# Layer 1's low halves placed 128 bytes further on in SBUF

## The chip, the cores and the metric

One core of one Trainium2 chip. The metric is the device time of one execution in microseconds, and of several runs their median.

## The reference, cut to what matters

Block-causal attention over 4 batches, 8 heads, 576 positions and head size 64; its output, 2,304 tokens of 512 channels, goes through two layers. Layer 1, where the change lies, is `h = x @ w_in` (512 to 2,048), softplus, and `@ w_out` (2,048 to 512):

```
attn = softmax(mask(q @ k.T / 8)) @ v
h = x @ w_in
g = maximum(h, 0) + log1p(exp(-abs(h)))
x2 = g @ w_out
```

Layer 2 (512 to 1,024 to 512, with a softmax-weighted unit and a layer norm between) follows on x2.

## The kernel before, in words

Every float32 operand of a layer's matrix product is split into a high half, rounded to float32r, and a low half, the rest. A product is then three matmuls into the same PSUM tile: high by high, high weights by low input, low weights by high input.

**Layer 1.** The tokens are cut into nine chunks of 256. For each chunk `Pair` works on two of the 16 blocks of 128 hidden columns at a time, 72 pairs in all. `Pair.a` (called twice) makes 12 matmuls each into `hp` with `w1` as the stationary and `xt` as the moving operand of 256 columns. ACT makes abs, exp and ln of it, DVE joins them (`stt`), a copy makes `gh`, and `do_gl` subtracts it to make `gl`. `Pair.b` (called twice) makes 12 matmuls each with `w2` as the stationary operand and `gh` or `gl` as the moving one, into `acc` (for chunk 1 into `R`). The loop of `Pair.a`, which `Pair.b` repeats with `gh`, `gl` and `w2`, is

```
for k in range(4):
    mm(hp[:, j], w[:, 0, k, :], x[:, 0, k, :], ...)
    mm(hp[:, j], w[:, 0, k, :], x[:, 1, k, :], ...)
    mm(hp[:, j], w[:, 1, k, :], x[:, 0, k, :], ...)
```

So of three matmuls the middle one moves a low half. Each matmul has a weight load of its own, and the load for the next matmul runs while the present one streams its columns. All matmuls are recorded at line 236, the helper `mm`.

**Order.** The order of all instructions on all engines is worked out when the program is built: `Plan` places tasks on the engines by rank, estimated duration and due time. The change touches no task, no duration and no rank, so the order stays.

**Stages.** Up to about 100 us: attention over the first 256 positions of the first batches (`UnitA`), the loading and unpacking of layer 1's weights (`Piece`, from `raw`), and what pairs of the first chunks these let through. To about 200 us: the rest of the first two chunks and of `UnitA`. To about 465 us: attention over the other positions (`UnitC`) between the pairs of the next chunks. To about 561 us: the last pairs, with layer 2's first blocks among them. To the end: layer 2 (`Tok`), whose matmuls move 512 columns, the last 48 of them 256.

**Places.** The tile pools are stacks in each partition's bytes. On the left side, from low to high: `w` (all layer weights but the first four blocks of `w1`), `l1` (`t`, `gh`, `gl`, `stg`, small ones), `xt` (three buffers of 8,192 bytes) and `wx` (the first four blocks of `w1`). Small unused tiles (`pad_x`, `pad_l`, spare columns of `gcol`) shift what follows. The places that come out of this, in bytes of a partition: `w1` from 4,224 and from 161,664, `w2` from 53,376, 102,528 and 110,976, `gh` at 123,968 and 126,016, `gl` at 128,064 and 130,112, `xt` at 137,024, 145,216 and 153,408. All blocks within them step by multiples of 512.

Call the *distance* of a matmul the start of the weights that are loaded while it streams (those of the next matmul) less the start of what it moves, modulo 256 bytes. Weights of layer 1 start at 128 modulo 256, and all that moves at 64, so the distance is 64 in every matmul of layer 1. In layer 2 the moving operands (`u1`, and `w1` tiles that hold the second matrix) and the stationary ones start at the same residue: distance 0.

Of the kernel before, what the change touches and what calls it, by code (L numbers as in the profile page):

```python
# [10 lines left out]
F32 = mybir.dt.float32  # L11
F32R = mybir.dt.float32r
# [54 lines left out]
CT = 256  # L67
# [159 lines left out]
def body(ctx: ExitStack, tc: tile.TileContext, qk, qkA, vP, vA, w1, w2, u1, u2, gln, out):  # L227
# [3 lines left out]
    XTB, LAG = 3, 3  # L231
# [21 lines left out]
    def pool(name, side, **kw):  # L253
        return tc.tile_pool(name=name, bufs=1, side=side, reuse_waits="tile", **kw)
# [4 lines left out]
    pl1 = left.enter_context(pool("l1", "left"))  # L259
    early, xts = ExitStack(), ExitStack()  # L260
    pxt = xts.enter_context(pool("xt", "left"))
    px = early.enter_context(pool("wx", "left"))
    qsh = psl.enter_context(pool("qh", "left", space=PSUM))
    state = {}
# [68 lines left out]
    xt = {}  # L333

    def xt_of(c):
        if c not in xt:
            xt[c] = pxt.tile([128, 2, 4, CT], F32R, tag="xt", name="xt", bufs=XTB)
            if len(xt) == XTB:
                pxt.tile([128, 16], F32, name="pad_x")
        return xt[c]  # L340
# [14 lines left out]
    class UnitC:  # L355
# [169 lines left out]
        def x_hi(self, c, off, done, w, e):  # L525
            copy(e, xt_of(c)[:, 0, self.pr, off:off + w], self.xn[:, done:done + w])
# [6 lines left out]
    class UnitA:  # L533
# [131 lines left out]
        def x_hi(self, e):  # L665
            copy(e, xt_of(self.b)[:, 0, self.pr, :], self.o)
# [7 lines left out]
    class Pair:  # L674
# [65 lines left out]
            copy(e, self.gh, self.t)  # L740

        def do_gl(self):
            self.gl = pl1.tile([128, 2, CT], F32R, tag="gl", name="gl", bufs=2)
            DVE.tensor_sub(self.gl, self.t, self.gh)  # L744

# [80 lines left out]
    def open_q():  # L826
        psl.close()
        state["qtr"] = left.enter_context(pool("qtr", "left", space=PSUM))
        pl1.tile([128, 24], F32, name="pad_l")

    NR, NCA = 3, 4
    t_open = add("POOL", 500, 0.0, open_a, ())
# [11 lines left out]
    def w_of(t, i):  # L844
        return lambda: t[:, i]
# [7 lines left out]
    for kind, f in todo:  # L853
        src, t, done = (w1[f], w1t[f], w1ready) if kind == "w1" else (w2[f * 128:f * 128 + 128, :], w2t[f], w2ready)
        p = Piece(src, w_of(t, 0), w_of(t, 1))
# [17 lines left out]
    def u1_of(i, f):  # L873
        return lambda: state["u1"][i][:, :, f * 128:f * 128 + 128]
# [4 lines left out]
    for f in range(8):  # L879
        p = Piece(u1[f], u1_of(0, f), u1_of(1, f))  # L880
# [4 lines left out]
    for f in range(8):  # L885
        p = Piece(u2[f * 128:f * 128 + 128, :], w_of(w1t[6 + f], 0), w_of(w1t[6 + f], 1), gcol[:, f:f + 1])
        n = len(upieces) % 3
        plan.at_group("U2", f)
        p.plan(upieces, 0.0, conv_u, 3 if f > 2 else n + 1, 3 if f > 2 else n + 1, [t_u, t_2], w1_free(6 + f))
        u2d.append(p.t_lo)  # L890
    t_q = add("PE", 1, 0, open_q, evacs[NCH - 1] + [pairs[-1].t_b1, t_u])
    t_w = add("DVE", 1, 0, open_3, [pairs[-1].t_a1, t_2])

# [225 lines left out]
```

## Time and profile before

| | |
|---|---|
| median of 3 runs | 753.29 us (751.56 to 753.55) |
| the profiled execution, its own time | 751.01 us |
| its span, first to last instruction | 749.2 us |
| matmuls | 5,368, of them 3,456 of layer 1 with 256 columns |
| mean granted clock of TensorE | 0.998 |

The span is the time from the first to the last instruction; the profiled execution's own time has 1.8 us around it. PE is TensorE's matmuls, PEld its weight loads; the ends of matmuls are modelled, so it is the step from one start to the next, or the length of a run of back-to-back matmuls in the chain of waits, that tells what one costs.

### The profile page before, as it was taken

What the parts mean: (1) busy time and instruction counts of PE and PEld (TensorE: products, weight loads), DVE (VectorE), ACT (ScalarE), POOL (GpSimd) and SP (SyncE); (2) the same over time, 40 slices, a digit from 0 to 9 for tenths busy, and PEclk for the clock granted to TensorE, in tenths of its full rate; (3) what the DMA queues carried; (4) which work ended last, traced back from release to release, by engine and by line L of the source; (5) the groups of instructions that cost most, each with busy time, mean ns of one, the idle gap of its engine ahead of it and who ended that gap; (6) DMA issues with size and microseconds to landing.
All of it is one profiled execution on the core that took longest, in us unless ns stands there. A gap on an engine that the chain in (4) does not pass through costs nothing.

```text
span 749.2 us, 13919 instructions
## 1 busy us (share of the span) xinstructions
PE 728.7 (97%) x5368; PEld 648.0 (86%) x5368; DVE 580.7 (78%) x1185; ACT 421.6 (56%) x876; POOL 0.7 (0%) x6
## 2 busy tenths in 40 slices
PE   7789999999999999999999999999999999999998
PEld 4688999999988888888878889999998888888887
DVE  5999994367787878877677886765879998998882
ACT  5788874354777767676666764446642433333331
POOL 0000000000000000000000000000000000000000
PEclk9999999999999999999999999999999999999999
DMA  7666630102476687648667662316313554433332
GB/s 224 202 219 199 235 118 23 57 22 72 87 159 146 139 153 165 140 112 166 120 136 160 143 130 96 114 58 198 127 43 99 116 111 99 98 98 84 85 64 77
DMA packets 153762, 91.66 MB, mean 122 GB/s; under 512 B 123360, under 2 KB 136928, under 8 KB 153696
## 3 DMA queue, kind: packets, MB, share of 16 engines
q1 hardware_dynamic: 153696, 90.77, 48.3%
q8 instruction: 42, 0.69, 0.4%
q14 instruction: 24, 0.20, 0.1%
HBM read 51.91 MB, written 9.48 MB: 82 GB/s over the span
## 4 chain that ended last, share of the span: by engine, by line
PE 71%; DVE 11%; DMA 11%; ACT 3%; SPq 3%; issue 2%; DVEq 0%; ACTq 0%
PE hp L236 17%; PE acc L236 16%; PE op L236 13%; PE h L236 13%; DMA raw<-in_w_dram 4%; PE O L236 3%; PE S L236 3%; DMA eC<-hl 3%; PE R L236 2%; DMA sums<-dT 2%; DVE ps L507 1%; DMA rC<-sums 1%; DVE a L313 1%; SPq L484 1%; PE r L236 1%
## 5 line engine op out<-in xcount | busy, mean ns | idle before, releaser
L236 PE MATMUL hp<-xt,w 128*128 128x256 f32 x1728 | 216.2, 281 | 0.9 <-DVE t L736 0.9
L236 PEld LDWEIGHTS hp<-xt,w 128*128 128x128 f32 x1728 | 206.2, 189 | 7.0 <-issue 4.9
L236 PE MATMUL acc<-gh,w 128*128 128x256 f32 x768 | 145.1, 281 | 0.0
L236 PEld LDWEIGHTS acc<-gh,w 128*128 128x128 f32 x768 | 121.1, 188 | 3.9 <-issue 3.4
L236 PE MATMUL acc<-gl,w 128*128 128x256 f32 x384 | 106.9, 278 | 0.3 <-DVE gl L744 0.3
L236 PE MATMUL h<-u,w 128*128 128x512 f32 x432 | 100.5, 389 | 0.0
L236 PE MATMUL op<-w,w2w 128*128 128x512 f32 (+1 forms) x456 | 100.5, 378 | 0.0
L236 PEld LDWEIGHTS op<-w,w2w 128*128 128x128 f32 x456 | 82.5, 188 | 16.0
L236 PEld LDWEIGHTS h<-u,w 128*128 128x128 f32 x432 | 80.9, 188 | 16.6
L727 ACT ACTIVATE t<-hp 128x512 f32<-128x512 f32 x72 | 42.7, 594 | 62.8 <-PE hp L236 53.2
L236 PEld LDWEIGHTS acc<-gl,w 128*128 128x128 f32 x384 | 72.2, 188 | 0.6 <-DVE gl L744 0.5
L736 DVE SCALAR_TENSOR_TENSOR t<-hp,t 128x512 f32<-128x512 f32 x72 | 49.1, 681 | 28.6 <-ACT t L733 28.4
L465 ACT ACTIVATE eC<-S,mC 128x384 f32<-128x384 f32 (+2 forms) x80 | 51.9, 651 | 24.6 <-DVE mC L457 24.2
L507 DVE COPY ps<-eC 128x1536 uint16<-128x1536 uint16 (+2 forms) x48 | 46.0, 958 | 23.0 <-DMA eC<-hl 22.8
L744 DVE TENSOR_TENSOR gl<-t,gh 128x512 fp32r<-128x512 f32 x72 | 49.5, 688 | 2.4 <-ACT gh L242 1.1
L457 DVE TENSOR_REDUCE mC<-S 128x2 f32<-128x768 f32 (+2 forms) x48 | 46.9, 978 | 2.4 <-PE S L236 1.0
L236 PE MATMUL acc<-gh,w2w 128*128 128x256 f32 x256 | 48.0, 281 | 0.0
L733 ACT ACTIVATE t<-t 128x512 f32<-128x512 f32 x72 | 45.5, 632 | 1.6
L730 ACT ACTIVATE t<-t 128x512 f32<-128x512 f32 x72 | 45.5, 632 | 1.6
L242 ACT ACTIVATE hl<-e 128x1024 uint16<-128x1024 uint16 x18 | 19.0, 1056 | 39.3 <-DVE e L980 39.3
L236 PEld LDWEIGHTS acc<-gh,w2w 128*128 128x128 f32 x256 | 40.2, 188 | 1.0 <-issue 0.7
L242 ACT ACTIVATE hl<-eC 128x1024 uint16<-128x1024 uint16 (+2 forms) x45 | 38.7, 860 | 0.6
(171 smaller groups left out, 1049.3 us busy)
## 6 DMA issues: line engine op xcount, KB each, us to landing
raw<-in_w_dram SPq DMA_DIRECT2D x32, 512.0 KB
qkC<-in_qk_dram SPq DMA_DIRECT2D x16, 480.0 KB
raw_u<-in_u_dram SPq DMA_DIRECT2D x11, 512.0 KB
v<-in_vP_dram SPq DMA_DIRECT2D x16, 320.0 KB
x2s<-stg SPq DMA_DIRECT2D x18, 256.0 KB
xr<-x2s SPq DMA_DIRECT2D x18, 256.0 KB
qkA<-in_qkA_dram SPq DMA_DIRECT2D x16, 256.0 KB
out_dram<-ob SPq DMA_DIRECT2D x15, 256.0 KB
```

Of the source, the lines that this page charges most:

```text
L236: PE.matmul(out, lhsT, rhs, start=start, stop=stop, skip_group_check=True)
L242: ACT.activation(out, a, AF.Copy)
L313: DVE.scalar_tensor_tensor(out=self.a, in0=self.raw[:, :, 0], scalar=29, in1=self.a, op0=ALU.logical_shift_right, op1=ALU.bitwise_or)
L457: DVE.tensor_reduce(out=self.m[:, i:4:2] if i < 2 else self.m[:, 4:5], in_=self.scores(i), axis=AX.X if i < 2 else AX.XY, op=ALU.max, nega ...
L465: ACT.activation(e, sc, AF.Exp, bias=self.m[:, c], accum_out=self.den[:, c])
L484: SP.dma_start(out=to[:, 0:256].rearrange("p (i q) -> p i q", i=2), in_=rs[2 * j:2 * j + 2].partition_broadcast(64))
L507: DVE.tensor_copy(dst, src)
L727: ACT.activation(self.t, self.hp, AF.Abs)
L730: ACT.activation(self.t, self.t, AF.Exp, scale=-1.0)
L733: ACT.activation(self.t, self.t, AF.Ln, bias=1.0)
L736: DVE.scalar_tensor_tensor(out=self.t, in0=self.hp, scalar=0.0, in1=self.t, op0=ALU.max, op1=ALU.add)
L744: DVE.tensor_sub(self.gl, self.t, self.gh)
```

## The change

The three buffers of `xt` become 2,112 words instead of 2,048, with the low half starting at word 1,056: 4,224 bytes behind the high half instead of 4,096. A 128-byte tile is put in front of `gl`, so both its buffers lie 128 bytes further on. `pad_l` grows by 128 bytes too, so that `xt` and `wx` move by multiples of 256. No instruction is added, removed, moved or given another shape.

```
@@ xt_of
         if c not in xt:
-            xt[c] = pxt.tile([128, 2, 4, CT], F32R, tag="xt", name="xt", bufs=XTB)
+            x = pxt.tile([128, 2112], F32R, tag="xt", name="xt", bufs=XTB)
+            xt[c] = x.rearrange("p (h x) -> p h x", h=2)[:, :, 0:1024].rearrange("p h (k t) -> p h k t", k=4)
@@ Pair
         def do_gl(self):
+            if "pad_g" not in state:
+                state["pad_g"] = pl1.tile([128, 32], F32, name="pad_g")
             self.gl = pl1.tile([128, 2, CT], F32R, tag="gl", name="gl", bufs=2)
@@ open_q
-        pl1.tile([128, 24], F32, name="pad_l")
+        pl1.tile([128, 56], F32, name="pad_l")
```

## Rows read from the trace of the kernel before

**Rows 1.** The page: busy time of PE, and the granted clock in 40 slices

```profile
PE 728.7 (97%) x5368; PEld 648.0 (86%) x5368; DVE 580.7 (78%) x1185; ACT 421.6 (56%) x876; POOL 0.7 (0%) x6
...
PEclk9999999999999999999999999999999999999999
```

**Rows 2.** Busy time by stretch: stretch, length, PE, PEld, DVE, ACT, POOL, clock, DMA, GB/s

```profile
44.00:100.00 56.00, 54.49 (x472) 50.94 (x471) 54.05 (x120) 45.73 (x97) 0.00 (x0) 1.00 0.65 215
100.00:200.00 100.00, 99.93 (x858) 95.08 (x859) 60.55 (x143) 51.68 (x127) 0.00 (x0) 1.00 0.18 52
200.00:465.00 265.00, 261.00 (x2156) 228.30 (x2155) 206.37 (x401) 179.98 (x370) 0.00 (x0) 1.00 0.64 139
465.00:580.00 115.00, 115.00 (x876) 109.78 (x875) 86.28 (x152) 57.57 (x96) 0.00 (x0) 1.00 0.35 108
```

**Rows 3.** The chain of waits, 40 to 100 us: start, length, what

```profile
47.70 4.35 DMA raw<-in_w_dram
...
53.26 4.47 DMA raw<-in_w_dram
```

**Rows 4.** The chain of waits, 100 to 205 us

```profile
107.34 1.38 PE acc L236 x12
...
117.85 2.72 PE hp L236 x24
...
130.51 1.41 PE R L236 x12
131.93 2.83 PE acc L236 x24
134.75 8.48 PE R L236 x72
143.24 5.65 PE hp L236 x48
...
150.40 1.56 PE hp L236 x12
```

**Rows 5.** The chain of waits, 465 to 580 us

```profile
467.30 2.72 PE acc L236 x24
...
524.42 2.72 PE hp L236 x24
527.14 5.45 PE h L236 x24
532.59 2.83 PE acc L236 x24
535.42 2.83 PE hp L236 x24
...
554.99 5.66 PE acc L236 x48
```

**Rows 6.** Weight loads and matmuls of layer 1, grouped by shape, 138 to 149 us

```profile
L236 PE MATMUL hp<-xt,w 128*128 128x256 f32 x48 | 5.8, 281 | 0.0
L236 PEld LDWEIGHTS hp<-xt,w 128*128 128x128 f32 x48 | 5.7, 189 | 0.0
```

**Rows 7.** The same groups, 470 to 536 us

```profile
L236 PE MATMUL hp<-xt,w 128*128 128x256 f32 x271 | 32.7, 277 | 0.0
L236 PEld LDWEIGHTS hp<-xt,w 128*128 128x128 f32 x271 | 31.6, 188 | 0.0
```

**Rows 8.** The chain of waits, the last layer-2 matmuls (512 columns; the last 48 have 256)

```profile
707.52 5.44 PE op L236 x24
...
718.40 27.52 PE op L236 x144
```

**Rows 9.** The page's costliest groups: who writes the low halves of the activations

```profile
L744 DVE TENSOR_TENSOR gl<-t,gh 128x512 fp32r<-128x512 f32 x72 | 49.5, 688 | 2.4 <-ACT gh L242 1.1
```

## The prediction

> **What bounds the kernel now.** I read the page first: TensorE's matmuls are busy 97% of the span, at the full granted clock in every slice [rows 1], so nothing in what follows comes from the clock. Then the busy times by stretch: PE is busy 54.5 of 56 us before 100 us, then 99.9 of 100, 261 of 265 and 115 of 115 [rows 2]. That a busy PE also ends the waits has to be read from the chain of waits. Before 100 us the chain runs through the weights' loads, 4.4 us at a time [rows 3]; from 100 us it is made mostly of matmuls of layer 1 [rows 4, 5].
>
> The third thing to see is in the lengths of these pieces. A run of 24 layer-1 matmuls takes either 2.72 us or 2.83 us: 113.3 or 117.9 ns for the same shape, engine and clock [rows 4, 5]. From 467.30 to 524.42 us every piece is a 2.72; after a block of 512-column matmuls (5.45 us) pieces of the same two kinds are 2.83 [rows 5]. So there are two paces, a short step and a long one, and once entered a pace lasts until the stream is broken. The grouped views say the same: where the long step holds, a matmul of `hp` is recorded with 281 ns and a weight load with 189 [rows 6], against 277 and 188 where the short one does [rows 7]. The weight loads are longer too, which points to the load of the next weights and the streaming operand getting into each other's way.
>
> There is one row for another distance. The last 144 matmuls of layer 2, at distance 0, take 27.52 us [rows 8]. Their 96 with 512 columns cost 5.44 / 24 = 226.7 ns each [rows 8], 21.76 us, which leaves 5.76 us for the 48 with 256 columns: 120.0 ns each. For the same shape, then: 113.3 or 117.9 ns at distance 64, 120.0 at distance 0.
>
> **The change part by part.** It adds no instruction, DMA or wait, and the order is built from the same numbers; no queue is passed. What moves is where three things lie.
>
> *The pads.* `pad_g` and the larger `pad_l` shift `xt` by 256 bytes; three `xt` buffers, each 256 larger, shift `wx` by 1,024. High halves thus keep residue 64 and all weights 128, and layer 2's places keep theirs. Cost: nothing.
>
> *The writers.* `gl` is written by the same DVE instruction, 688 ns on average [rows 9], 128 bytes further on and still on a multiple of 64; the same holds for the low half of `xt` and for the staging tile that a DMA reads. I take 0. If a row off its place cost as much as the step between the two paces (4%), 72 writes would lose 2 us of DVE time, which lies beside PE: DVE is busy 206 of 265 us and 86 of 115 [rows 2].
>
> *The distance.* With high halves at residue 64 and low ones at 192, the three matmuls of a group have distances 64, -64 and 64. So it is one step in three that changes. No row shows a distance of -64. Its cost is bounded from both sides by the paces seen: 113.3 ns below and 120.0 above [rows 5, 8]; nothing below 113.3 is supported, since 512 columns take 226.7 ns, twice 113.3 [rows 8], although a weight load covers at most half of that stream. So 113.3 looks like the streaming rate itself.
>
> *What there is to gain.* Only long steps that stand on the chain count. From 100 us on, the chain's pieces of 12 or a multiple are 59 with 1,200 matmuls under 115.5 ns (first 107.34, last 524.42 [rows 4, 5]), 22 with 564 matmuls at 116 to 118 ns (first 130.51, last 554.99 [rows 4, 5]) and 23 pieces with 372 matmuls that contain a restart (as 1.56 us for 12, at 150.40 [rows 4]). The long ones cost (2.83 - 2.72) / 24 = 4.6 ns each above the short, so 564 x 4.6 = 2.6 us. The restarts stay: their excess, 1.56 - 1.36 = 0.2 us, is one gap. Long steps before 100 us lie beside the loads [rows 3]: 0. If PE gets ahead between 200 and 465 us, it next waits for the attention's DMA and DVE work, since 4 us of idle are left there already [rows 2]; of the 2.6 us only 0.6 come from that stage (132 matmuls), and I do not cut it further.
>
> **The forecast.** I take the change to break the long pace, not the short one: the long pace must sustain itself from matmul to matmul through equal distances, whereas a step of another distance in each group moves the load against the stream. Against the profiled execution's own 751.01 us (1.8 us outside the span), the sum is 751.0 - 2.6 = 748.4. That execution is 2.3 us under the median of the runs shown, and 0.5 under the lowest. Part of that spread may itself be how often the long pace was entered; if so it shrinks along with it. I put the median at 749.0. This case alone spans 745.8 (748.4 less another 2.6, if long steps that now stand beside the chain were as many and came to count) to 751.
>
> **The rivals.**
>
> *No change within the noise.* About 0.3% (2.3 us) is what a measurement of this kernel can tell from none, as its own spread of 2.0 us shows. Either the pace is set at each restart, by chance, and does not depend on the distance, or -64 acts as 64 does. For it: the same two paces appear in `hp`, `acc` and `R` alike [rows 4], which have different tiles and places; and the short pace lasts from 467 to 527 us over all of them [rows 5]. Against: 120.0 at distance 0 [rows 8]. The time: 752 to 754. A change that missed its aim belongs here as well, since only every third step differs. The Trainium skill speaks for this rival (TensorE: Matmul & The Clock Gate, Part 2, "What happens when you issue a matmul"): loading the next tile's weights is said not to take SBUF read bandwidth from the running matmul. By that rule places would not matter and the time would stay at 753.3; the two step lengths at one shape [rows 5] don't agree with it.
>
> *Slower: the short pace loses its footing.* The mechanism is that a load at distance -64 collides where one at 64 did not, in the middle matmul of each group, and that the late load pushes the stream into the long pace, where it stays. Its place is the 1,200 short steps of the chain; its price 4.6 ns each, 5.5 us: 751.0 + 5.5 = 756.5. At the upper bound, all 1,764 at 120.0 ns: 1,200 x 6.7 + 564 x 2.1 = 9.2 us, so 760. It decides as soon as more than 564 of the 1,764 steps (32%) are long, today's share. For it: the short pace does get lost, after the 512-column block at 527 us [rows 5], and the one other distance with a row has the longest step. Against: 60 us of unbroken short pace (467 to 527 us) show that it stands a good deal.
>
> **How the numbers follow.** Broken long pace 0.46 (749.0), no change 0.27 (753), slower 0.27 (756.5 to 760, of which 0.17 near the lower). Faster by over 0.3% is below 751.0, slower is above 755.6. The range reaches from 745.8 to 760, both ends being the bounds above, as cases of either sign have weight; it leaves out about 1 in 8.
>
> **What would show it.** Right: pieces of 24 layer-1 matmuls in the chain at 2.72 us nearly everywhere, also in 532 to 561 us, where now all are 2.83 [rows 5]; loads of `hp` at 188 ns between 138 and 149 us [rows 6]; the 120 ns at the end unchanged. Wrong: pieces of 2.83 or 2.88 us where there were 2.72, above all in the stretch from 467 to 527 us; or the same mix as before. A total that moves while the piece lengths do not would mean that something other than the distance, a wait on DVE or a DMA, did it.

## The result, and the profile after

The changed kernel is slower: 758.39 us (median of 6, 755.83 to 759.9) against 752.36 us for the kernel before in the same comparison (749.23 to 753.55). The ratio is 1.0086, with a 95% interval of 1.0058 to 1.0115. The time lies inside the predicted range, but the forecast was a faster kernel. The profiled executions say the same: 758.02 us with a span of 756.2, against 751.01 and 749.2, so 7.0 us more.

All matmuls stand in the same order as before, TensorE's clock is granted in full in every slice, and the busy times of DVE and ACT agree with those before to 0.5 us. What grew is PE. From the page of the kernel after, to be held against [rows 1] and [rows 9]:

```profile
PE 737.7 (98%) x5368; PEld 656.4 (87%) x5368; DVE 581.1 (77%) x1185; ACT 422.1 (56%) x876; POOL 0.7 (0%) x6
...
PEclk9999999999999999999999999999999999999999
...
L747 DVE TENSOR_TENSOR gl<-t,gh 128x512 fp32r<-128x512 f32 x72 | 49.5, 687 | 2.5 <-ACT gh L242 1.3
```

PE has 9.0 us more, its weight loads 8.4 us more. The writer of the moved `gl` still takes 687 ns: moving what it writes costs nothing.

The chain of waits of the kernel after, 465 to 580 us (start, length, what), answers to [rows 5]:

```profile
468.08 2.83 PE hp L236 x24
470.91 2.83 PE acc L236 x24
...
507.65 2.83 PE hp L236 x24
510.48 2.84 PE acc L236 x24
...
517.80 6.06 DMA xr<-x2s
...
528.36 2.98 PE acc L236 x23
531.33 2.83 PE hp L236 x24
534.16 5.44 PE h L236 x24
539.60 2.83 PE acc L236 x24
...
562.00 5.65 PE acc L236 x48
```

Every unbroken piece of 24 layer-1 matmuls is 2.83 us (one 2.84), where it was 2.72 up to 524 us. The block of 512-column matmuls is as before (5.44). Counted by the prediction's rule (pieces of 12 or a multiple, from 100 us on), the chain holds no piece under 116 ns a matmul; before it held 59 with 1,200 matmuls. Taken from the starts of the matmuls, the back-to-back steps now average 117.8 ns. That is the mean of the old long pace, but not its pattern: the steps repeat every six, as 115, 122, 117, 117, 118, 118 or as 114, 118, 118, 120, 118, 118 ns. The long pace before averages 117 or 118 at each of six places.

**Where the 7.0 us are.** I lined up the starts of the same matmuls in both traces; the order is the same, so each has its partner. "Lost" is how much later the kernel after is at the end of the stretch than at its start. "Steps" is what the back-to-back steps of layer 1 take over 113.33 ns, after less before.

| stretch, us | lost | from steps |
|---|---|---|
| to 48.8 | -1.0 | 0.2 |
| to 100 | 1.1 | 0.6 |
| to 200 | 0.7 | 1.15 |
| to 466 | about 2.6 | 4.75 |
| to 543 | 3.4 | 2.4 |
| to the end | 0.0 | 0 |
| sum | about 6.8 | 9.1 |

From 200 to 466 us nearly half of the loss is given back. The busy times by stretch show where, in the kernel after, beside [rows 2]:

```profile
200.00:465.00 265.00, 262.89 (x2134) 230.07 (x2133) 205.71 (x400) 178.53 (x366) 0.00 (x0) 1.00 0.65 137
465.00:580.00 115.00, 114.47 (x875) 110.05 (x874) 81.37 (x144) 57.65 (x96) 0.00 (x0) 1.00 0.34 108
```

PE stood idle for 4.0 us of the 265 before and stands idle for 2.1 now, which fits a PE that comes later and waits less for what comes from elsewhere. In the last stretch of layer 1 it is the other way round: 0.53 us of new idle time. The chain shows a detour there, a 6.06 us transfer of `xr` (layer 2's first input), and ACT's split of it stands ahead of a pair's abs. The timeline of ACT in the kernel after (start, busy, engine, line, what, idle before it and its cause):

```profile
523.94 0.63 ACT L242 ACTIVATE w<-xr 128x512 fp32r<-128x512 f32 x1 [2.09 <-DMA xr<-x2s]
```

This stretch lost 1.0 us more than its back-to-back steps explain, and all of it lies in three steps around the waits for that pair's `gh` and `gl`. From the timeline of PE:

```profile
527.63 0.38 PE L236 MATMUL acc<-gh,w 128*128 128x256 f32 x1 [0.19 <-DVE gh L244]
528.36 0.38 PE L236 MATMUL acc<-gl,w 128*128 128x256 f32 x1 [0.34 <-DVE gl L747]
```

From start to start these three take 468, 728 and 222 ns, where the same three took 113 or 114 before: 1.08 us, of which the profile shows 0.53 as idle time.

### The profile page after: what moved, and what is told of

It is laid out like the page before. It is cut to its first block, busy times and chain, and to the rows that moved or that the text cites. A ratio compares the mean times of both kernels' runs of the same rounds, so it can differ in the third digit from the quotient of the medians.

```text
span 756.2 us, 13919 instructions
## 1 busy us (share of the span) xinstructions
PE 737.7 (98%) x5368; PEld 656.4 (87%) x5368; DVE 581.1 (77%) x1185; ACT 422.1 (56%) x876; POOL 0.7 (0%) x6
## 4 chain that ended last, share of the span: by engine, by line
PE 88%; DMA 5%; DVE 3%; ACT 1%; SPq 1%; issue 1%; DVEq 0%; ACTq 0%
PE hp L236 25%; PE acc L236 22%; PE op L236 13%; PE h L236 13%; PE S L236 5%; PE O L236 5%; PE R L236 4%; DMA raw<-in_w_dram 2%; PE r L236 2%; DMA eC<-hl 1%; DMA xr<-x2s 1%; ACT eA L618 1%; PE r L644 1%; DMA rC<-sums 1%; DMA qkA<-in_qkA_dram 0%
## 5 line engine op out<-in xcount | busy, mean ns | idle before, releaser
L236 PE MATMUL hp<-xt,w 128*128 128x256 f32 x1728 | 220.8, 283 | 1.4 <-DVE t L737 1.4
L236 PEld LDWEIGHTS hp<-xt,w 128*128 128x128 f32 x1728 | 210.4, 189 | 7.4 <-issue 5.1
L236 PE MATMUL acc<-gh,w 128*128 128x256 f32 x768 | 148.4, 283 | 0.2 <-DVE gh L244 0.2
```

What stands on the lines that cost most here:

```text
L236: PE.matmul(out, lhsT, rhs, start=start, stop=stop, skip_group_check=True)
```

## The experiments

Sixteen kernels ran. In all of them the work and its order stay as before and only places change; each edit is against the kernel before. The tables give the ratio to the kernel before on the same chip, its 95% interval, and how many layer-1 matmuls stand in short pieces (under 115.5 ns each) of the chain from 100 us on, by the prediction's rule (1,200 in the kernel before). Each count is that of one execution, the profiled one.

### The pads alone, and each half of the change alone

`e1_pads` keeps every pad and buffer size of the change, but the low halves stay at residue 64:

```
+            x = pxt.tile([128, 2112], F32R, tag="xt", name="xt", bufs=XTB)
+            xt[c] = x[:, 0:2048].rearrange("p (h k t) -> p h k t", h=2, k=4)
...
             DVE.tensor_sub(self.gl, self.t, self.gh)
+            if "pad_g" not in state:
+                state["pad_g"] = pl1.tile([128, 32], F32, name="pad_g")
```

> All pads of the change and its larger xt buffers, but both low halves stay at residue 64, so every distance in layer 1 stays 64. Theory M (the mixed distances are the cause): as the kernel before, both paces present, runs of 24 matmuls at 2.72 us in the stretch from 467 to 527 us, ratio to before 0.997 to 1.003. Rival P (the shifted buffers are the cause, whatever the distance): as the changed kernel, every run of 24 at 2.83 us, ratio 1.007 to 1.011.

`e2_a_only` has only the edit in `xt_of`, `e3_g_only` only `pad_g` and the larger `pad_l`.

> Only the low halves of xt are moved by 128 bytes; gh and gl keep distance 64. Theory M in its strict form (a pace lasts until the stream is broken, so the matmuls of xt pass their long step on to those of gh and gl that follow at once): every run of 24 at 2.83 us, ratio 1.007 to 1.011. Theory M in its local form (a step's length follows from its own distances): hp at 2.83 us, acc at 2.72 us, ratio 1.000 to 1.004. Rival P: as e1.

> Only gl is moved by 128 bytes. Strict form of M: every run of 24 at 2.83 us, ratio 1.007 to 1.011. Local form: acc at 2.83 us, hp at 2.72 us, ratio 1.000 to 1.004. If only one of the two halves of the change mattered, this run and the one with xt alone would differ by more than 0.005 in their ratios.

| run | median, us | ratio | interval | in short pieces |
|---|---|---|---|---|
| e1_pads | 751.90 | 1.0001 | 0.9979 to 1.0022 | 1,176 |
| e2_a_only | 755.64 | 1.0052 | 1.0036 to 1.0068 | 216 |
| e3_g_only | 754.99 | 1.0058 | 1.0036 to 1.0079 | 420 |

So the pads cost nothing that shows and the moved low halves cost the rest. Each half alone costs more than half of the whole (0.52% and 0.58%, together 1.10% against 0.86%), so the two don't add up. Neither form of the expectation has the ratio of these two runs: the strict one said 1.007 to 1.011, the local one 1.000 to 1.004. The chain of `e1_pads` also holds the detour over `xr`:

```profile
500.94 2.72 PE hp L236 x24
503.66 2.73 PE acc L236 x24
...
510.48 5.80 DMA xr<-x2s
...
523.67 2.72 PE hp L236 x24
```

There it costs 0.96 us, in the same three steps (347, 728 and 223 ns), and the kernel as a whole is no slower, so the detour is not what makes the change slow. The chain of `e3_g_only`, where `hp` has the one distance throughout and `acc` the mixture:

```profile
470.54 2.73 PE hp L236 x24
473.26 2.82 PE acc L236 x24
476.08 2.73 PE hp L236 x24
...
517.64 2.82 PE acc L236 x24
520.46 2.73 PE hp L236 x24
...
531.66 2.83 PE hp L236 x24
534.49 5.44 PE h L236 x24
```

Here the two cases stand side by side in one run of PE without a gap: the mixture takes 2.82 us and the unmixed groups come back to 2.73 every time. So a mixture need not throw the stream out of the short pace. It is not so everywhere. Over the same stretch of `e2_a_only`, where `acc` is the unmixed one, both are long:

```profile
499.17 2.83 PE acc L236 x24
502.00 2.83 PE hp L236 x24
```

Take all places where a group of `hp` and one of `acc` or `R` (11 matmuls or more of each) follow each other without a gap. The unmixed group is short in 44 of 92 such pairs in `e3_g_only` and in 31 of 92 in `e2_a_only`; in the kernel before, both are short in 69 of 93. So a mixed half comes with two costs, its own time and fewer short unmixed groups, which fits halves that don't add up. Whether the mixture takes the short groups away or the restarts, which the shifted buffers also change, is not shown.

### One distance for everything

These shift all that moves in layer 1 by the same bytes: `pad_t` ahead of `t`, and `pad_x` filled up to 256 bytes. For 128 bytes, a distance of -64:

```
+            if "pad_t" not in state:
+                state["pad_t"] = pl1.tile([128, 32], F32, name="pad_t")
             self.t = pl1.tile([128, 2, CT], F32, tag="t", name="t", bufs=2)
...
-                pxt.tile([128, 16], F32, name="pad_x")
+                pxt.tile([128, 48], F32, name="pad_x")
```

`e5_all_0`, `e6_all_32`, `e7_all_96` and `e8_all_128` have 16, 8, 56 and 48 words in `pad_t`. `e11_all_48` and `e12_all_80` instead view wider tiles of `gh`, `gl` and `xt` from their 4th and 60th word on.

> All that moves in layer 1, high and low, is shifted by 128 bytes: every distance is -64 (192), none differs from the next. Theory M: the short pace is there again, at least half of the runs of 24 at 2.72 us, ratio 0.996 to 1.004. Rival D (a distance of -64 collides by itself): no run of 24 under 2.80 us, 2.83 to 2.88 us, ratio 1.007 or more (2.88 us everywhere would be 1.02).

> Every distance of layer 1 is 0, as in layer 2. Theory S (with equal distances both paces exist, and the distance decides which one a restart falls into): at distance 0 none falls into the short one, every run of 24 at 2.88 us as in the last 48 matmuls of layer 2, ratio about 1.015 (some 2,000 short steps on the chain and beside it, 6.7 ns each, part of it hidden). Theory U (any uniform distance has the same two paces of 2.72 and 2.83 us): no run over 2.84 us, ratio under 1.011.

> Every distance of layer 1 is 32. Theory S: the share of short steps differs from that at 64 (66%) and from that at -64 (about 10%), and lies between those at 0 and at 64. Theory U: both paces and a share of its own by chance; 2.72 and 2.83 us alone. A distance at which every restart falls into the short pace would give 0.993 to 0.995.

> Every distance of layer 1 is 96. Theory S: as for 32, on the other side of 64; if 64 is the middle of a favourable stretch, fewer short steps than there, ratio 1.002 to 1.01; if the stretch goes on, more of them, 0.993 to 0.999. Theory U: 2.72 and 2.83 us alone.

> Every distance of layer 1 is 128, half way between 64 and -64. Theory S: a share of short steps between those two, 10% to 66%, ratio 1.000 to 1.009. If distances repeat with 128 bytes, as at 0: 2.88 us a run of 24 and about 1.015.

> Every distance of layer 1 is 48. If the short pace needs exactly 64: no run of 24 at 2.72 us, between the 2.83 us at 64 and the 2.84 us at 32, ratio 1.008 to 1.010. If 64 lies in a favourable stretch: runs at 2.72 us, with a share of their own; a share above the 66% at 64 would give under 1.000, all of them 0.993.

> Every distance of layer 1 is 80. As for 48, on the other side: exactly 64 needed, no run at 2.72 us and 1.005 to 1.010; a favourable stretch, runs at 2.72 us, 0.993 to 1.004.

The paces are mean steps between starts, in blocks of 12 layer-1 matmuls:

| distance | run | paces, ns | median, us | ratio | interval |
|---|---|---|---|---|---|
| 0 | e5_all_0 | 120.0 | 763.48 | 1.0164 | 1.0137 to 1.0190 |
| 32 | e6_all_32 | 118.3 | 758.62 | 1.0103 | 1.0072 to 1.0133 |
| 48 | e11_all_48 | 116.65, 119.2 | 760.80 | 1.0109 | 1.0089 to 1.0129 |
| 64 | e1_pads | 113.3, 117.8 | 751.90 | 1.0001 | 0.9979 to 1.0022 |
| 80 | e12_all_80 | 119.2 | 762.56 | 1.0135 | 1.0120 to 1.0151 |
| 96 | e7_all_96 | 117.3, 118.7 | 758.28 | 1.0091 | 1.0061 to 1.0121 |
| 128 | e8_all_128 | 118.7, 120.0 | 761.13 | 1.0132 | 1.0106 to 1.0157 |
| -64 | e4_all_minus64 | 113.3, 117.8 | 758.46 | 1.0092 | 1.0072 to 1.0111 |

The same 72 matmuls into `R`, one piece of the chain in each run, at distances 32, 48, 80, 96 and 128 (in the kernel before 8.48 us [rows 4]):

```profile
136.67 8.52 PE R L236 x72
137.04 8.40 PE R L236 x72
135.02 8.59 PE R L236 x72
135.66 8.55 PE R L236 x72
135.18 8.64 PE R L236 x72
```

The time follows the pace: 120.0 gives 1.0164, 119.2 gives 1.0135, 118.3 gives 1.0103. The chain of `e5_all_0`, and that of `e4_all_minus64`:

```profile
507.51 2.88 PE hp L236 x24
510.39 2.88 PE acc L236 x24
```

```profile
505.23 2.83 PE hp L236 x24
508.06 2.83 PE acc L236 x24
```

Distance -64 has the same two paces as 64. But only 192 of its matmuls stand in short pieces: most of its restarts ended in the long one. So a uniform -64 costs as much as the mixture (1.0092 against 1.0086). Nothing of what was tried lies under 113.3.

`e5_all_0` came out as one of its cases had it; most of the others did not. `e4_all_minus64` was to have at least half of its runs of 24 at 2.72 us, or none under 2.80. The expectations for 32, 96 and 128 counted on the two paces known so far, in some share, or on a repeat of 0; each of these distances has a pace of its own, though the ratio at 96 lies where one case had it. At 48 and 80 no run of 24 took 2.72, as the case of exactly 64 had it, but 80 cost more than the 1.010 that this case allowed.

### Other mixtures

`e9_reversed_mix` has -64, 64, -64 in each group (`pad_t` of 32 words on top of the change), `e15_low_256` puts the low halves 256 bytes further on, `e16_low_64` 64 bytes (64, 0, 64), each with pads that keep the rest. `e14_xt_minus64` moves both halves of `xt` by 128 bytes and leaves `gh` and `gl`, so that `acc` has 64 throughout and `hp` -64:

```
-        pl1.tile([128, 24], F32, name="pad_l")
+        pl1.tile([128, 56], F32, name="pad_l")
...
-                pxt.tile([128, 16], F32, name="pad_x")
+                pxt.tile([128, 48], F32, name="pad_x")
```

> High halves at distance -64, low halves at 64: the changed kernel's mix turned round. Theory M, local form (a group with two distances has no short pace, each group of three loses about 13 ns, whichever distance is the odd one): every run of 24 at 2.83 us, repeating every six matmuls, ratio 1.007 to 1.011. Rival D2 (the low half at -64 is what costs): runs of 24 at 2.72 us come back, ratio under 1.005.

> Both halves of xt are at distance -64, gh and gl at 64: uniform within every group of 12 or 24, another one in the next group. If only the mix within a group of three costs: runs of 24 at 2.72 and at 2.83 us and nothing repeating every six, ratio 1.000 to 1.009 by what the restarts pick. If any change of distance costs, also between groups: every run of 24 at 2.80 us or more, and steps of 114 to 122 ns side by side after each change.

> Low halves 256 bytes further on instead of 128: the distances modulo 256 stay 64 throughout, modulo 512 they mix as in the change. If distances count modulo 256 (or a divisor): as before, 0.997 to 1.003, 113 and 118 ns alone. If modulo 512 or more: steps of 114 to 122 ns mixed, repeating every six, ratio 1.007 to 1.011.

> Low halves 64 bytes further on: the middle step of each group at distance 0, the other two at 64. If the loss belongs to mixing two distances: no run of 24 at 2.72 us, all of one length at or over 2.83 us, ratio 1.007 to 1.016. If each step has the cost of its own distance: one step in three at 120 ns and the others at 113 or 118, on average 115.6 or 118.5; runs of 24 at 2.77 and 2.84 us, ratio 1.003 to 1.008.

| run | median, us | ratio | interval | in short pieces |
|---|---|---|---|---|
| e9_reversed_mix | 758.01 | 1.0078 | 1.0061 to 1.0096 | 0 |
| e14_xt_minus64 | 756.87 | 1.0065 | 1.0041 to 1.0090 | 456 |
| e15_low_256 | 753.07 | 1.0000 | 0.9979 to 1.0021 | 1,008 |
| e16_low_64 | 760.43 | 1.0122 | 1.0086 to 1.0159 | 0 |

Two pieces of the chain of `e15_low_256`, and two of `e16_low_64`:

```profile
517.88 2.72 PE acc L236 x24
520.60 2.72 PE hp L236 x24
```

```profile
117.36 2.83 PE hp L236 x24
241.66 2.86 PE acc L236 x24
```

At 256 bytes nothing happens, so it is the place modulo 256 that counts, not that the low half was moved; a shorter period is out, since 128 bytes do cost. Both mixtures of 64 and -64 average 117.8 ns; 64, 0, 64 gives 117.8 in some stretches and about 119.2 in others, against 115.5 or 118.5 as a sum of uniform paces. These runs came out as one of their cases had it, `e16_low_64` in its ratio but with two lengths. The chain of `e14_xt_minus64`:

```profile
459.25 2.73 PE acc L236 x24
461.98 2.83 PE hp L236 x24
464.81 2.73 PE acc L236 x24
...
525.89 2.73 PE acc L236 x24
528.62 2.83 PE hp L236 x24
531.45 5.47 PE h L236 x24
536.91 2.83 PE acc L236 x24
```

This run tells most. With -64 in all of `hp`, `hp` takes the long pace and `acc` the short one, in turns, for 70 us without a gap. Yet -64 alone does have a short pace, and 64 a long one. Side by side without a gap, `hp` is long and `acc` or `R` short in 66 pairs, both are long in 27, and `hp` is short in none; in `e4_all_minus64` and in the kernel before the two are always both short or both long. So a stream carries something from group to group. I call it a phase and read from the pairs that the one that is short at 64 is long at -64; what it is no run shows.

### The same distances at other places

`e13_all_places_128` moves weights and moving operands of both layers by 128 bytes, distances kept; `e10_layer2_64` changes layer 2 alone, to 64 and -64 instead of 0:

```
+    pw.tile([128, 32], F32, name="pad_w")
     w1t = [(px if
...
-pu1.tile([128, 24], F32, name="pad_u")
+pu1.tile([128, 56], F32, name="pad_u")
```

```
-    lln, lhn = wide[0][:, 64:], wide[1]
+    lln, lhn = wide[0][:, 16:2064], wide[1][:, 16:2064]
...
+        pu1.tile([128, 16], F32, name="pad_v")
```

> Weights, inputs and activations of both layers are all 128 bytes further on, so every distance is as before (64 in layer 1, 0 in layer 2). If the distance counts: both paces as before, runs of 24 at 2.72 us between 467 and 527 us, ratio 0.997 to 1.003. If the place of what moves counts (residue 192 instead of 64): as with everything at -64, hardly a run of 24 at 2.72 us, ratio 1.006 to 1.011.

> Layer 1 as before; layer 2's moving tiles and its left operands are shifted so that its distances are 64 and -64 instead of 0. If 113.3 ns for 256 columns is the rate of the stream itself: the 512-column blocks stay at 5.44 us for 24 and only the last 48 matmuls get shorter, 120.0 to 117.8 or 113.3 ns, 0.1 to 0.3 us; ratio 0.998 to 1.001. If 512-column matmuls at distance 0 pay for their weight loads too (their 13 ns over 512 columns at the granted clock): 24 of them in 5.25 to 5.40 us, at 840 matmuls 1 to 6 us, ratio 0.992 to 0.999. The pace that the layer-1 matmuls take up after such a block at 532 us may change as well.

| run | median, us | ratio | interval | in short pieces |
|---|---|---|---|---|
| e13_all_places_128 | 755.22 | 1.0047 | 1.0026 to 1.0068 | 420 |
| e10_layer2_64 | 755.05 | 1.0043 | 1.0025 to 1.0062 | 1,380 |

In `e13_all_places_128` both paces are there, at 113.3 and 117.8. In layer 1 this can't tell the distance from the place of what moves, since `e4_all_minus64` has the same two paces with its moving operands at the same residue, 192. Layer 2, shifted as a whole, keeps its paces too (226.7 ns at 512 columns, 119.8 in the last 48); what decides is `op` in `e10_layer2_64`, below. The stretch of layer 1 that began at 457 us took the long pace this time, which the distance case of the expectation did not have, and the ratio lies between its two cases:

```profile
506.38 2.83 PE hp L236 x24
509.21 2.83 PE acc L236 x24
```

Which pace a restart picks is thus not set by the distance alone. The places of the attention's tiles against the weights changed too in this run; that was not separated.

Nor is it drawn afresh each time. From 100 us on, 52 unbroken stretches of layer-1 matmuls begin at the same matmul in all runs with distance 64 throughout layer 1. The last 11 steps of each tell its pace, and 38 of the 52 are short in the kernel before. `e1_pads` has the same pace as that kernel in 50 of them, `e15_low_256` in 48, `e10_layer2_64` in 45, though these are other programs, run on three chips; with as many short ones spread by chance it would be about 32. `e13_all_places_128`, on the same chip as `e15_low_256`, agrees in 22, where chance would give about 24. So something that the first three programs share with the kernel before, and that the shift of all places changes, goes into the pace at a restart.

The end of the chain of `e10_layer2_64`, beside [rows 8]:

```profile
712.07 5.60 PE op L236 x24
717.67 5.59 PE h L236 x24
723.26 28.07 PE op L236 x144
```

At 512 columns it is distance 0 that is better: 5.60 / 24 = 233 ns against 226.7. The last 48 matmuls, with 256 columns, step by 117.8 instead of 120.0, which gives back 0.1 us. Both cases of the expectation had the 512-column blocks as fast as before or faster. Layer 1 has no fewer short pieces than before (1,380); of the 5.4 us between the two profiled executions 4.3 come after 560 us, where layer 2 is alone. In `op` what moves (`w1t`) has kept its place and only the stationary operand lies 64 bytes further on. So a matmul's pace is not a matter of what moves alone: it is the place of the one against the other that counts.

No run beat the kernel before; `e1_pads` and `e15_low_256` equal it.

## Why the prediction was wrong

*What held.* The pads and the writers were taken at nothing: `e1_pads` has 1.0001, and `gl` takes 687 ns against 688. The bounds for the unknown distance, 113.3 to 120.0 ns, held for the mean, which is 117.8; single steps reach 122. The restarts, the clock and the last 144 matmuls (27.52 us in both) stayed. The path was the right one too: from 100 us on PE's steps set the time, and where the stretch from 200 to 466 us gave nearly half of the loss back, it was in the idle 4 us that the prediction named.

*The step that failed* is the forecast's choice: "I take the change to break the long pace, not the short one". Nothing in the rows decided between the two, and the two that bore on it, the short pace lost after the 512-column block and 120.0 ns at the one other distance, stood under the rival. So the term of 2.6 us to be saved came out as 9.1 us of longer steps to be paid. The argument, that the long pace sustains itself through equal distances, holds for the short pace just as well, since it too had been seen only at equal distances. What the runs show in its place is in two parts. The long pace is not a disturbance that another distance shakes off: distance -64 has it as well (`e4_all_minus64`), and the change leaves nothing under it. And the short pace is not a streaming rate that any good distance reaches: the phase in which a group at 64 is short makes a group at -64 long (`e14_xt_minus64`). I read from this that a mixture has no phase in which it is short throughout. The price of the mixture, though, does not come out of the paces as a sum: two steps at 113.3 and one at 117.8 would average 114.8 ns, and 117.8 is measured, with six-step patterns that reach 122. Two of six matmuls move at -64, but five of six steps are over 116 ns, so steps at 64 are hit too. What happens inside the chip at these starts no run here shows.

*The rival "the short pace loses its footing"* had the place right and came close in the price, the latter in part by luck. It put all 1,200 short steps of the chain at 4.6 ns each, 5.5 us, and 756.5. Measured are 0 short pieces, 7.0 us in the profiled executions and 6.0 between the medians. The parts differ: 9.1 us of longer steps (the chain's count left out pieces that were no multiple of 12 and everything before 100 us), about 2.2 us given back between 200 and 466 us, some 1.0 us lost around the waits that follow `xr`, and a start that was 1.0 us quicker by 48.8 us. Its picture, a stream pushed into the long pace where it stays, is not borne out in `e3_g_only`, where the unmixed groups are short again at once; in `e2_a_only` they stay long over the same stretch, and whether the mixture or the restart did that is open.

*The rival "no change"* fell with 1.0058 as the lower end of the interval. One of its two grounds, a pace set at each restart by chance, falls too: programs of the same distance take the same pace at 45 to 50 of 52 restarts. The rule that this rival leaned on (the Trainium skill, "TensorE: Matmul & The Clock Gate", Part 2, "What happens when you issue a matmul": loading the next weights takes no SBUF read bandwidth from the running matmul) does not agree with these runs: one shape at one clock takes 113.3 to 120.0 ns by the places of its operands, and in `op` of `e10_layer2_64` moving the stationary operand alone takes a 512-column step from 226.7 to 233 ns.

*What stays open.* What decides the pace that a restart takes. It repeats from program to program, yet at the same distances the short pieces hold 1,200 matmuls of the chain in the kernel before and 420 in `e13_all_places_128`, and 192 in `e4_all_minus64`, where the same two paces exist. So the case that a new arrangement loses short restarts belongs to any forecast of this kind, and the one here had no such term. All weights of layer 1 lie at one residue, so whether the next weights or the present ones matter was not separated either.

## What to carry to other kernels

Where the chain of waits is made of matmuls of one shape and its pieces come in two lengths, write down for each the place of the next weights less that of the moving operand, modulo 256 bytes, before moving anything: here that difference alone was worth up to 1.6% of the kernel. Try the few uniform values at the shape in question (64 was best at 256 columns; of 0, 64 and -64, 0 at 512), don't mix two of them in a stream, and don't add up the paces of uniform streams for a mixed one. An equal distance is no safeguard by itself: -64 throughout cost as much as the mixture. If a forecast hangs on which of two paces seen a disturbance destroys, look for a row in which it has already happened; if there is none, give both sides the same chance.

## What the runs showed of the hardware

- A matmul of 256 float32r columns with its own weight load, at the full granted clock, steps by 113.3 to 120.0 ns, by the distance between the next weights and what moves (the table above): 120.0 at 0, two paces of 113.3 and 117.8 at 64 and at -64, nothing below 117 at 32, 80, 96 and 128. With 512 columns it is 226.7 ns at 0 and 233 at 64.
- Once taken, a pace lasts until the stream is broken: at distance 64 or -64 throughout (the kernel before, `e1_pads`, `e4_all_minus64`, `e10_layer2_64`, `e13_all_places_128`, `e15_low_256`) no stretch of 36 steps or more changes it after its first dozen steps. It can outlast groups of another pace in between: 2.73 and 2.82 us in turns in `e3_g_only` from 465 to 528 us, 2.73 and 2.83 in `e14_xt_minus64`. From 531 us in the one, and after the 512-column block at 531 us in the other, all pieces shown are 2.83.
- The pace that a restart takes repeats: 45 to 50 of 52 restarts agree between the kernel before and three other programs with distance 64, and 22 of 52 once all places are shifted by 128 bytes.
- 16 bytes matter: 48 and 80 cost 1.1% and 1.35% against 64. 256 bytes don't: 1.0000.
